# Transposing normalized activations in square blocks on VectorE and through memory instead of on TensorE, in two layers of attention and feed-forward

## The chip, the cores and the metric

The kernel runs on one core of a Trainium2 chip. The engines are TensorE (PE, with its weight loads PEld), VectorE (DVE), ScalarE (ACT), GpSimd (POOL) and SyncE (SP, which issues most transfers here). The metric is the device time of one execution in microseconds, lower is better. All sizes below are in fp32.

## The reference

Two rounds of attention and a SwiGLU feed-forward, each behind a layer normalization and with a residual. There are S = 2048 tokens of D = 448 features; 16 heads of 28 features share one key and one value (multi-query); the feed-forward is 1792 wide.

```
def _A_ref(x, wq, wk, wv, wo):
    q = (x @ wq).reshape(B, S, 16, 28).transpose(0, 2, 1, 3)
    k, v = x @ wk, x @ wv
    scores = einsum("bhqd,bkd->bhqk", q, k) * 28 ** -0.5
    o = einsum("bhqk,bkd->bhqd", softmax(scores), v)
    return o.transpose(0, 2, 1, 3).reshape(B, S, 448) @ wo
def _B_ref(x, w_gate, w_up, w_down):
    return (silu(x @ w_gate) * (x @ w_up)) @ w_down
for _ in range(2):
    x = x + _A_ref(layernorm(x), ...)
    x = x + _B_ref(layernorm(x), ...)
```

## The kernel before

**Layout.** The residual stream `xres` stays on the chip: 128 partitions (tokens) by 16 tiles by 448 features. Four tiles make a chunk `c` of 512 tokens. Normalization gives `xn`, tokens on partitions; the products need features on partitions, so each chunk is transposed ("turned"). A number is held as a high part and a remainder (`xh`, `xl`; so are weights, `wgh` and `wgl`, `wdh` and `wdl`), and most products are three matmuls. The fourth block of features is half empty; its upper 64 partitions hold a remainder, and for the feed-forward a second copy `xd` holds the high part there.

**The turn.** `norm_steps` (L207 to L230) gives nine steps for a chunk: statistics of four tiles, one reciprocal root on GpSimd, and four normalizations on VectorE (L226, 128x448 each). `flip` (L238) then runs, for each of four blocks of features, four transpositions of 128x128 on PE (L243) into one PSUM bank, and `flipped` (L246) copies the bank to `xh` on ScalarE (L249, L256, L257) and subtracts to `xl` on VectorE (L250, L259). With four chunks, two layers and two products that is 16 turns of 16 transpositions, 256 in all.

**The order.** The order in which the program is written is each engine's order. The names of the stages, with the times of layer 0:

- *Projection* (`project` L458, `q` L478): sixteen products (`product_T` L261, eleven matmuls each, L269), four a chunk. Each result goes through ScalarE (`stage`) to memory (`qd`, `kt`); VectorE transposes the piece that holds V (L502); after every fourth, `maxima` (L390) bounds the scores, with its own matmuls (L395) and VectorE steps (L397 to L406).
- *Attention* (`scores` L525): 16 groups of four heads (i = 0 to 15, chunk i // 4), each of 16 steps kt over the key tiles. A step has the score matmuls (L562), two exponentials on ScalarE (L568 for one head, L569 for three) and the products with V (L599). The stacked queries of group i + 2 are brought by `stack` (L372, kt = 4), split by `parts` (kt = 7) and completed by `rows` (kt = 9), into one of three buffers `qstack`. At kt = 10 of groups 4, 8 and 12 `between_steps` (L572) does the output projection (`outproj` L541) of the chunk before: 48 matmuls. In groups 8 and 12, halves of the turn of chunk 0 (for the feed-forward) stand among them.
- *Feed-forward* (`FeedForward`, `unit` L788): the hidden width is seven groups of two blocks (`gi`, `n`), and each block runs over four chunks: 56 units in each layer, 112 in all. A unit has 21 pairs of gate and up matmuls on two halves of the array (L289) in two halves, A and B; the SiLU on ScalarE (L822), the product with `up` on VectorE (L823), the high part on ScalarE (L824), its remainder on VectorE (L827). Between A and B stands the first half of the unit before's `down` (L699, six pairs), and behind B the second. Half B starts when ScalarE has copied one column of A's banks (`between` L293, tile `seen`). `accumulate` (L728) adds the finished sums of a chunk to `xres`: two on VectorE (L736), two by a ScalarE copy to `stage` (L739) and a GpSimd addition (L740).
- *Around the feed-forward's start* (`rest` L853): chunk 1 is turned behind the last output projection, chunks 2 and 3 in halves inside units (`mid`: at gi = 0, (c, n) = (1, 1) and (2, 1)).
- *Around its end* (`hand_over` L754): as soon as a chunk is finished its statistics are taken and, through the list `soon` (each entry counts units), its normalization. Chunks 0 and 1 are turned for the next attention inside the units of chunks 2 and 3, the first three projections run behind units, and the rest behind the last one, with the turns of chunks 2 and 3.

Two tiles with one buffer link these: `xn`, and `sg`, which the SiLU and `maxima` both use.

Of the kernel before, what the change touches and what calls it, by code (L numbers as in the profile page):

```python
# [8 lines left out]
F32 = mybir.dt.float32  # L9
# [6 lines left out]
P = 128  # L16
# [13 lines left out]
LEAD = 4  # L30
# [23 lines left out]
def forward(  # L54
# [28 lines left out]
    xpool = ctx.enter_context(tc.tile_pool(name="xpool", bufs=1))  # L83
# [47 lines left out]

    def split(hi, lo, raw):
        nc.gpsimd.tensor_scalar(hi, raw, 1.0, 0.0, ALU.mult, ALU.add)
        nc.gpsimd.tensor_tensor(lo, raw, hi, ALU.subtract)
# [9 lines left out]
    qts = [pers.tile([P, 2, 512], F32R, name=f"qstack{n}") for n in range(3)]  # L144
# [62 lines left out]
    def norm_steps(c, pool=pers):  # L207
# [14 lines left out]
        def apply(t):  # L222
            if t == 0:
                got["x"] = pool.tile([P, 4, 512], F32, name="xn")
            o, i, r = got["x"][:, t, 0:D], xres[:, 4 * c + t, :], got["r"][:, t : t + 1]
            nc.vector.tensor_scalar(o, i, mv[:, 4 * c + t, 0:1], r, ALU.subtract, ALU.mult)  # L226
# [3 lines left out]
        return fs + [lambda t=t: apply(t) for t in range(4)], got  # L230

    def norm(c, pool=pers):
        fs, got = norm_steps(c, pool)
        for f in fs:
            f()
        return got

    def flip(got, tiles, ks=range(4), place=None):  # L238

        for k in ks:  # L240
            pt = place if place is not None else bank(wide[-1])[1]
            for t in range(4):
                nc.tensor.transpose(pt[:, P * t : P * t + P], got["x"][:, t, P * k : P * k + P], ident)  # L243
            flipped(tiles, k, pt, nc.vector.tensor_copy if place is not None else nc.scalar.copy)
# [55 lines left out]
    class Attention:  # L300


        def __init__(self, layer):
# [12 lines left out]
            for i in range(3):  # L316
                self.at(4 + 3 * i, lambda i=i: self.stack(i))
                self.at(6 + 3 * i, lambda i=i: self.parts(i))
                if not full:
                    self.at((10, 12, 13)[i], lambda i=i: self.rows(i))  # L320
            if not full:
                self.at(2, self.first_keys)
                self.at(3, self.diagonal)
            for i in range(len(GR) if full else 0):
                fs, place = self.max_steps(i)
                if i == 1:
                    fs[KC] = lambda f=fs[KC]: (f(), self.places[0]())
# [51 lines left out]
        def parts(self, i):  # L379
            q = qts[i % 3]  # L380
            split(q[:, 0, :], q[:, 1, :], qraw)

        def rows(self, i):
# [3 lines left out]
            dst = qts[i % 3][28:125:32, :, :].rearrange("j z (b w) -> j (z b) w", w=32)  # L387
# [31 lines left out]
        def max_steps(self, i):  # L419

            got = {}
            q = qts[i % 3]
# [86 lines left out]
        def finish(self):  # L509
# [12 lines left out]
            self.advance(len(self.steps), NM + KC * LEAD)  # L522
            wide.append(LOW)

        def scores(self, ff):  # L525
            next(switch)
            with tc.tile_pool(name=f"at{self.layer}", bufs=1, reuse_waits="tile") as wp:
# [13 lines left out]
                def outproj(c, t, po, gs=range(NG)):  # L541
                    oh, ol = on[c]
                    ts_ = slice(P * t, P * t + P)
                    for g in gs:
                        for z, (a, b) in enumerate(((oh, woh), (oh, wol), (ol, woh))):
                            nc.tensor.matmul(  # L546
                                po[:, 0:D], a[:, g, ts_], b[:, g, :], start=(g + z == 0), stop=(g == NG - 1 and z == 2)
# [6 lines left out]
                def step(n):  # L554
# [3 lines left out]
                    q, k, ks = qts[i % 3], keys[kt // 4], slice(P * (kt % 4), P * (kt % 4) + P)  # L558
# [13 lines left out]
                def between_steps(n):  # L572
# [3 lines left out]
                    if full:  # L576
                        self.lent = free[:, 0, :]
                        self.advance(KC)
                        if kt == 11 and i + 1 < len(GR):
# [4 lines left out]
                    ks = list({8: (0, 1), 12: (2, 3)}.get(i, ()))  # L584
# [54 lines left out]

                X0 = xtile(xpool)  # L640
                fs, got = norm_steps(0)
                fs1, got1 = norm_steps(1)
                ff.norms[1] = got1
                ff.second = norm_steps(2)
# [318 lines left out]
```

## Time and profile before

| | |
|---|---|
| median of 3 runs | 2031.24 us (2031.08 to 2032.20) |
| the profiled execution's own time | 2031.19 us |
| its span in the trace | 2029.5 us |
| start and first projection | 0 to 64 us |
| attention 0 | 64 to 586 |
| feed-forward 0 | 586 to 1043 |
| second projection | up to 1070 |
| attention 1 | 1070 to 1592 |
| feed-forward 1 and the end | 1592 to 2029.5 |

Busy time in the whole span, from the page:

```profile
PE 2011.8 (99%) x18631; PEld 1274.4 (63%) x18631; DVE 460.7 (23%) x892; ACT 1310.3 (65%) x2152; POOL 535.6 (26%) x599
```

A row of the timeline has the start in the span, the duration, the engine, the line, the operation, the tile written and those read, the shape, a count (rows that follow each other are joined), and in brackets the idle time before it with what ended it. A row of one line's view has the count, the least, median and greatest duration in ns, the first and last start, and the shapes. A row of the windows has start and end, the length, then the busy time and count of PE, PEld, DVE, ACT and POOL, the granted clock, the DMA share and GB/s. PE counts as busy whenever a matmul is under way, so its 99% in the attention doesn't say that it sets the pace there.

### The profile page before, as it was taken

Reading aid. Unit: us, or ns where it says so; the run is one execution under the profiler, and the core shown is the slowest. Engines: PE = TensorE matmul, PEld = TensorE weight load, DVE = VectorE, ACT = ScalarE, POOL = GpSimd, SP = SyncE. Lnnn points to the kernel's source line nnn. Section 1 sums busy time; section 2 is a strip of 40 time slices with the busy share of each in tenths; the row PEclk is TensorE's granted clock in tenths of the full one; section 3 lists DMA queues with packets and bytes.
Section 4 is the critical chain, followed back from the end, with each engine's and each line's share of the span. In section 5 each row is a group of like instructions: output and inputs, shape, how many; then the busy total and the mean of one; then the engine's idle time right before and its main releaser. Section 6 shows DMA issues by size and latency. Waiting matters only on the chain.

```text
span 2029.5 us, 43649 instructions
## 1 busy us (share of the span) xinstructions
PE 2011.8 (99%) x18631; PEld 1274.4 (63%) x18631; DVE 460.7 (23%) x892; ACT 1310.3 (65%) x2152; POOL 535.6 (26%) x599
## 2 busy tenths in 40 slices
PE   9999999999999999999999999999999999999998
PEld 7433434334358999999883343343343689988886
DVE  7200101002115232322451001010011232232322
ACT  4899797997964333333349998979979543333332
POOL 4222211032312333333351221211232123233320
PEclk9999999999999999999999999999999999999999
DMA  5111000011100111100031010000110000111101
GB/s 162 51 30 30 12 22 12 20 28 30 28 12 19 31 31 31 31 25 18 22 99 39 20 30 12 22 12 22 31 47 9 28 16 16 31 31 31 31 1 74
DMA packets 76512, 63.44 MB, mean 31 GB/s; under 512 B 22904, under 2 KB 63224, under 8 KB 76312
## 3 DMA queue, kind: packets, MB, share of 16 engines
q1 hardware_dynamic: 75896, 60.33, 10.8%
q8 instruction: 147, 2.41, 0.5%
q14 instruction: 53, 0.43, 0.1%
q10 hardware_dynamic: 416, 0.26, 0.0%
HBM read 47.72 MB, written 12.32 MB: 30 GB/s over the span
## 4 chain that ended last, share of the span: by engine, by line
PE 48%; ACT 47%; DVE 2%; issue 1%; DMA 1%; POOL 0%; SPq 0%; ACTq 0%; DVEq 0%; POOLq 0%
PE bank L289 39%; ACT pt L569 31%; ACT pt L568 15%; PE bank L269 3%; PE three L546 2%; PE bank L546 2%; PE bank L243 1%; PE bank L599 0%; PE three L562 0%; DMA qd<-stage 0%; DVE xl L250 0%; DVE xn L226 0%; DMA wq<-in_A_wq_dram 0%; DMA kt<-stage 0%; DVE vt L502 0%
## 5 line engine op out<-in xcount | busy, mean ns | idle before, releaser
L569 ACT ACTIVATE pt<-three 128x1536 f32<-128x1536 f32 x512 | 741.3, 1448 | 0.0
L599 PE MATMUL bank<-pt,vsb 128*32 128x512 f32 x4096 | 545.1, 604 | 0.5 <-ACT pt L569 0.5
L562 PEld LDWEIGHTS three<-qstack,keys 32*128 32x128 f32 x4608 | 252.2, 183 | 446.6 <-ACT pt L568 394.1
L562 PE MATMUL three<-qstack,keys 32*128 32x512 f32 x4608 | 497.2, 425 | 0.9 <-DVE vt L502 0.9
L562 PE MATMUL bank<-qstack,keys 32*128 32x512 f32 x1536 | 491.5, 425 | 0.4 <-ACT pt L568 0.4
L289 PE MATMUL bank<-xh,wgh 64*128 64x512 f32 x1728 | 445.3, 390 | 0.4
L289 PE MATMUL bank<-xh,wgl 64*128 64x512 f32 x1404 | 366.7, 390 | 0.0
L568 ACT ACTIVATE pt<-bank 128x512 f32<-128x512 f32 x512 | 306.1, 598 | 68.0 <-PE bank L562 66.7
L289 PE MATMUL bank<-xl,wgh 64*128 64x512 f32 x1296 | 333.3, 390 | 0.0
L289 PE MATMUL bank<-wdh,h 64*128 64x448 f32 x1792 | 330.6, 364 | 1.2 <-ACT h L824 0.8
L289 PEld LDWEIGHTS bank<-xh,wgh 64*128 64x128 f32 x1728 | 261.8, 184 | 18.8 <-DVE xl L250 1.5
L740 POOL TENSOR_TENSOR xres<-stage,xres 128x448 f32<-128x448 f32 x108 | 127.6, 1205 | 497.6 <-ACT stage L739 497.6
L633 POOL TENSOR_TENSOR o<-o 128x512 f32<-128x512 f32 x32 | 41.1, 1285 | 816.3 <-DMA o<-rd 710.5
L289 PEld LDWEIGHTS bank<-wdh,h 64*128 64x128 f32 x1792 | 242.1, 184 | 14.6 <-issue 2.7
L562 PEld LDWEIGHTS bank<-qstack,keys 32*128 32x128 f32 x1536 | 243.3, 183 | 1.1 <-ACT pt L568 1.0
L296 ACT COPY seen<-bank 128x1 f32<-128x1 f32 x664 | 81.5, 163 | 247.7 <-PE bank L289 245.3
L289 PEld LDWEIGHTS bank<-xh,wgl 64*128 64x128 f32 x1404 | 215.9, 184 | 13.7
L289 PE MATMUL bank<-wdl,h 64*128 64x448 f32 x896 | 216.5, 366 | 0.0
L822 ACT ACTIVATE sg<-bank 128x512 f32<-128x512 f32 x112 | 67.3, 601 | 219.7 <-PE bank L289 214.5
L289 PEld LDWEIGHTS bank<-xl,wgh 64*128 64x128 f32 x1296 | 195.6, 184 | 9.8
L599 PEld LDWEIGHTS bank<-pt,vsb 128*32 128x32 f32 x4096 | 80.8, 108 | 189.7 <-issue 174.9
L823 DVE TENSOR_TENSOR sg<-bank,sg 128x512 f32<-128x512 f32 x112 | 77.5, 692 | 500.0 <-ACT sg L822 491.0
(115 smaller groups left out, 1731.6 us busy)
## 6 DMA issues: line engine op xcount, KB each, us to landing
o<-rd SPq DMA_DIRECT2D x32, 256.0 KB
qd<-stage SPq DMA_DIRECT2D x32, 224.0 KB
qraw<-qd SPq DMA_DIRECT2D x128, 56.0 KB
wdr<-in_B_w_down_dram SPq DMA_DIRECT2D x28, 224.0 KB
wr<-in_B_w_gate_dram SPq DMA_DIRECT2D x28, 192.0 KB
wr<-in_B_w_up_dram SPq DMA_DIRECT2D x28, 192.0 KB
out_dram<-xres SPq DMA_DIRECT2D x15, 224.0 KB
xres<-in_A_x_dram SPq DMA_DIRECT2D x3, 896.0 KB
```

The costliest lines, as they stand in the source:

```text
L269: nc.tensor.matmul(po, a, b, start=(i == 0), stop=(i == len(seq) - 1))
L289: nc.tensor.matmul(po, a, b, start=start, stop=stop, skip_group_check=True)
L296: nc.scalar.copy(seen[:, i : i + 1], po[:, 0:1])
L546: nc.tensor.matmul(po[:, 0:D], a[:, g, ts_], b[:, g, :], start=(g + z == 0), stop=(g == NG - 1 and z == 2))
L562: nc.tensor.matmul(three[:, j, :] if j < 3 else one, k[js, kp, ks], q[js, part, :], start=(z == 0), stop=(z == 2), tile_position=(32 * j, 0),)
L568: nc.scalar.activation(pt1, one, AF.Exp, scale=SCALE)
L569: nc.scalar.activation(pt, three, AF.Exp, scale=SCALE)
L599: nc.tensor.matmul(accs[i][32 * j : 32 * j + 32, :], vsb[:, kt, :], pts[n][j], start=(kt == 0), stop=(kt == NT - 1), skip_group_check=True,)
L633: nc.gpsimd.tensor_tensor(rb, oraw, rb, ALU.mult)
L740: nc.gpsimd.tensor_tensor(r, s, r, ALU.add)
L822: nc.scalar.activation(sg, pg[0], AF.Silu)
L823: nc.vector.tensor_tensor(sg, pg[1], sg, ALU.mult)
```

## The change

- **The turn through VectorE and memory.** `norm_steps(c, True)` normalizes a tile into `sg`, and VectorE's transpose turns it in square blocks of 32 by 32 into `xn`, writing every fourth element (16 bytes), so that the four tiles interleave. `send` writes `xn` to memory in four pieces, which puts the blocks in their places, and `load` reads it back with features on partitions. `cut` makes `xh` and `xl` from that with the copies and subtractions of `flipped`, from SBUF instead of PSUM. It is used for all feed-forward chunks of both layers and for chunks 0, 1 and 2 of attention 1: 11 of the 16 turns. The four of attention 0 and chunk 3 of attention 1 stay on PE.
- **Where its steps stand.** For the feed-forward, chunks 0, 1 and 2 are normalized and sent in groups 5, 9 and 13 of the attention and loaded in the next group; 0 and 1 are also cut there, all on VectorE. Chunk 2 is cut in `rest`, chunk 3 goes through `soon` (one unit apart: normalize and send, load, cut). At the hand-over, chunks 0 and 1 go through `soon` in the same way, chunk 2 is loaded behind projection 4 and cut behind projection 6. Two projections run one unit later than before, the third behind the last unit. `mid` is gone.
- **Token order.** Inside a chunk, column 4 p + t now is token 128 t + p. The down products and the output projection take their tokens as every fourth column (`tokens`), and the remaining `flip` writes PSUM so.
- **Buffers.** Two `qstack` instead of three: the stack of group i + 1 is read at kt = 2, split at 5, completed at 9. Two buffers in `xpool` (chunks 0 and 1) instead of one, two in `xbp` instead of three.

The branch with `full` is not taken in the runs, and its edits are left out.

```diff
+    def tokens(cols, t):
+        return cols[:, t:512:4]
...
-    qts = [pers.tile([P, 2, 512], F32R, name=f"qstack{n}") for n in range(3)]
+    qts = [pers.tile([P, 2, 512], F32R, name=f"qstack{n}") for n in range(2)]
...
         def apply(t):
+            o = pers.tile([P, 512], F32, name="sg") if away else None
             if t == 0:
-                got["x"] = pool.tile([P, 4, 512], F32, name="xn")
-            o, i, r = got["x"][:, t, 0:D], xres[:, 4 * c + t, :], got["r"][:, t : t + 1]
+                got["x"] = pers.tile([P, 4, 512], F32, name="xn")
+            o = (o if away else got["x"][:, t, :])[:, 0:D]
+            i, r = xres[:, 4 * c + t, :], got["r"][:, t : t + 1]
             nc.vector.tensor_scalar(o, i, mv[:, 4 * c + t, 0:1], r, ALU.subtract, ALU.mult)
-            nc.gpsimd.tensor_copy(got["x"][:, t, D:512], o[:, 384:D])
+            if away:
+                nc.vector.transpose(side()[:, :, :, t], o.rearrange("p (k s) -> p k s", s=32))
+            else:
+                nc.gpsimd.tensor_copy(got["x"][:, t, D:512], o[:, 384:D])
+        def side():
+            return got["x"].rearrange("p t n -> p (t n)")[:, 0 : 4 * D].rearrange("p (k s t) -> p k s t", s=32, t=4)
+        def send():
+            turns.append(dram.tile([D, 512], F32, name=f"xt{len(turns)}"))
+            got["xt"] = turns[-1]
+            for a in range(4):
+                nc.sync.dma_start(
+                    got["xt"].rearrange("(k r) n -> r k n", r=32)[:, :, P * a : P * a + P],
+                    side()[32 * a : 32 * a + 32].rearrange("p k s t -> p k (s t)"),
+                )
+        def load():
+            got["raw"] = pers.tile([P, 4, 512], F32, name="xn")
+            rows3(got["raw"], got["xt"])
...
+    def cut(got, tiles, ks=range(4), copy=nc.scalar.copy):
         for k in ks:
-            pt = place if place is not None else bank(wide[-1])[1]
+            flipped(tiles, k, got["raw"][:, k, :], copy)
+    def flip(got, tiles):
+        for k in range(4):
+            pt = bank(wide[-1])[1]
             for t in range(4):
-                nc.tensor.transpose(pt[:, P * t : P * t + P], got["x"][:, t, P * k : P * k + P], ident)
-            flipped(tiles, k, pt, nc.vector.tensor_copy if place is not None else nc.scalar.copy)
+                nc.tensor.transpose(tokens(pt, t), got["x"][:, t, P * k : P * k + P], ident)
+            flipped(tiles, k, pt, nc.scalar.copy)
...
-                                po[:, 0:D], a[:, g, ts_], b[:, g, :], start=(g + z == 0), stop=(g == NG - 1 and z == 2)
+                                po[:, 0:D], tokens(a[:, g, :], t), b[:, g, :], start=(g + z == 0), stop=(g == NG - 1 and z == 2)
...
-                        if ks:
-                            flip(got, X0, [ks.pop(0)], one)
...
+                for c in range(3):
+                    ff.X[c] = xtile(xpool) if c < 2 else None
+                    fs, got = norm_steps(c, True)
+                    n = NT * (4 * c + 5)
+                    for kt, f in enumerate(fs):
+                        later[n + 6 + kt] = f
+                    later[n + 18] = got["load"]
+                    for k in range(4) if c < 2 else ():
+                        later[n + 22 + k] = lambda c=c, got=got, k=k: cut(got, ff.X[c], [k], nc.vector.tensor_copy)
...
-                    if kt == 4 and 2 < i + 2 < len(GR):
-                        self.stack(i + 2)
+                    if kt == 2 and i + 1 < len(GR):
+                        self.stack(i + 1)
...
-                                (a[rs, P * t : P * t + P], b[rs, :]),
+                                (tokens(a[rs, :], t), b[rs, :]),
...
             self.soon.append([1, ready])
-            if c < 2:
-                self.mid[len(groups) - 1, c + 2, 0] = [lambda ks=ks: flip(got, a.X[c], ks) for ks in ((0, 1), (2, 3))]
-                self.soon.append([2, lambda: [a.project() for _ in range(2 - c)]])
+            if c == 2:
+                a.plan[4, 1] = [got["load"]]
+                a.plan[6, 1] = [lambda: cut(got, a.X[c])]
+                return
+            self.soon.append([2, got["load"]])
+            self.soon.append([3, lambda: cut(got, a.X[c])])
+            if c == 0:
+                self.soon.append([4, lambda: (a.project(), a.project())])
+                self.soon.append([5, a.project])
...
-            self.turned(1)
-            fs2, self.norms[2] = self.second
-            fs3, self.norms[3] = norm_steps(3)
-            for f in fs2[5:] + fs3[:5]:
+            for c in (0, 1):
+                dma(self.xd[c][64:128, :], self.X[c][0][0:64, 3, :])
+                self.X[c] = (*self.X[c][:2], self.xd[c])
+            third, got = norm_steps(3, True)
+            for f in third[:5]:
                 f()
-            self.soon.append([1, lambda: [f() for f in fs3[5:]]])
             for c in (2, 3):
-                self.mid[0, c - 1, 1] = [lambda c=c, ks=ks: self.turned(c, ks) for ks in ((0, 1), (2, 3))]
+                self.X[c] = xtile(self.xbp, self.xd[c])
+            cut(self.norms[2], self.X[2])
+            self.soon.append([0, lambda: [f() for f in third[5:]]])
+            self.soon.append([1, got["load"]])
+            self.soon.append([2, lambda: cut(got, self.X[3])])
```

The order on VectorE at the end of feed-forward 0, from the last unit's remainder (`h`) to the additions of chunk 3's first two sums (`bank_6650` and `bank_6651` before, `bank_6688` and `bank_6689` after: the banks that the fifth and sixth projections then take), before:

```order
L827 TENSOR_TENSOR h_11683<-sg,h_11683 128x512
L226 TENSOR_SCALAR xn<-xres,mv,rstd 128x448 x4
L502 STREAM_TRANSPOSE vt<-bank_6646 32x512
L365 TENSOR_TENSOR kdiag<-few,mask 112x512
L736 TENSOR_TENSOR xres<-bank_6650,xres 128x448
L736 TENSOR_TENSOR xres<-bank_6651,xres 128x448
```

And in the change (the pair of L232 and L234 stands there four times, once a tile, and is shown once):

```order
L849 TENSOR_TENSOR h_11628<-sg,h_11628 128x512
L525 STREAM_TRANSPOSE vt<-bank_6687 32x512
L277 TENSOR_TENSOR xl<-xn,xh 128x512 x3
L286 TENSOR_TENSOR xh<-xn,xh 64x512
L232 TENSOR_SCALAR sg<-xres,mv,rstd 128x448
L234 STREAM_TRANSPOSE xn<-sg 128x448
...
L525 STREAM_TRANSPOSE vt<-bank_6684 32x512
L388 TENSOR_TENSOR kdiag<-few,mask 112x512
L762 TENSOR_TENSOR xres<-bank_6688,xres 128x448
L762 TENSOR_TENSOR xres<-bank_6689,xres 128x448
```

Chunk 1's four subtractions (L277, L286), four transposes (L234) and one more transpose of V have moved ahead of the two additions.

The order on ScalarE at the start of feed-forward 0, around the third chunk's turn; `bank_78` and `bank_79` are the sums of a finished chunk, the other banks those of gate, up and down. Before, the turn's copies stand behind the first `seen` copies inside the next unit, each half behind its transpositions on PE (the first half shown):

```order
L824 CAST h_7122<-sg 128x512
L739 COPY stage<-bank_78 128x448
L739 COPY stage<-bank_79 128x448
L296 COPY seen<-bank_6647 128x1
L296 COPY seen<-bank_6648 128x1
L249 CAST xh<-bank_6649 128x512
L249 CAST xh<-bank_6646 128x512
L296 COPY seen<-bank_6650 128x1
L296 COPY seen<-bank_6651 128x1
```

And in the change, behind the high part of the unit (gi, c, n) = (0, 2, 0), whose staging copies it also has:

```order
L844 ACTIVATE sg<-bank_6685 128x512
L846 CAST h_7123<-sg 128x512
L765 COPY stage<-bank_78 128x448
L765 COPY stage<-bank_79 128x448
L276 CAST xh<-xn 128x512 x3
L283 CAST xh<-xn 64x512
L284 CAST xd_6851<-xn 64x512
L323 COPY seen<-bank_6687 128x1
L323 COPY seen<-bank_6684 128x1
L323 COPY seen<-bank_6688 128x1
```

All five copies (L276, L283, L284) now stand in one place, ahead of the first `seen` copies of the next unit.

More of the change, by code (lines that the diff above doesn't have):

```diff
@@ L315, in __init__ @@
                 self.at(4 * c + 7, lambda c=c: self.key_split(c))
[L316 to L320, printed above, removed]
+            self.at(4, lambda: self.stack(0))
+            self.at(6, lambda: self.parts(0))
             if not full:
+                self.at(10, lambda: self.rows(0))
                 self.at(2, self.first_keys)
@@ L521, in finish @@
                     f()
-            self.advance(len(self.steps), NM + KC * LEAD)
+            self.advance(len(self.steps), NM)
+            if full:
+                self.places[0]()
             wide.append(LOW)
@@ L670, in scores @@
                         due.pop(n)()
-                    if i in (5, 13, 14) and kt > 5:
-                        for f in {5: fs, 13: fs1, 14: ff.second[0][:5]}[i][kt - 6 : kt - 5]:
-                            f()
+                    if n in later:
+                        later.pop(n)()
                 for n in (last - 2, last - 1):
@@ L906, in forward @@
         nc.sync.dma_start(xres[:, 4 * c : 4 * c + 4, :], xs[:, 4 * c : 4 * c + 4, :])
-    at.X = {c: xtile(xpool if c == 0 else xbp) for c in range(NC)}
+    at.X = {c: xtile(xpool if c < 2 else xbp) for c in range(NC)}
     parts[0]()
```

71 lines of the change are left out of this document (24 added, 47 removed).

## The prediction

> **What bounds the kernel now.** I read the page's chain first, then the busy time by stage, then the rows of single units. The page's lines on the chain that ended last:
>
> ```profile
> PE 48%; ACT 47%; DVE 2%; issue 1%; DMA 1%; POOL 0%; SPq 0%; ACTq 0%; DVEq 0%; POOLq 0%
> PE bank L289 39%; ACT pt L569 31%; ACT pt L568 15%; PE bank L269 3%; PE three L546 2%; PE bank L546 2%; PE bank L243 1%; PE bank L599 0%; PE three L562 0%; DMA qd<-stage 0%; DVE xl L250 0%; DVE xn L226 0%; DMA wq<-in_A_wq_dram 0%; DMA kt<-stage 0%; DVE vt L502 0%
> ```
>
> Two engines share the end: TensorE in the feed-forward (L289), ScalarE's exponentials in the attention (L568, L569). The transpositions (L243) are 1% of the chain, some 20 us. By stage (busy time of PE, PEld, DVE, ACT, POOL with counts; then clock, DMA share, GB/s):
>
> ```profile
> 64.00:586.00 522.00, 519.70 (x5286) 197.62 (x5284) 52.65 (x150) 487.65 (x515) 107.72 (x115) 1.00 0.09 23
> 643.00:984.00 341.00, 341.00 (x3083) 337.18 (x3083) 102.53 (x150) 114.00 (x419) 120.60 (x102) 1.00 0.10 27
> 984.00:1043.00 59.00, 58.63 (x410) 46.08 (x407) 32.06 (x66) 23.78 (x66) 19.30 (x34) 1.00 0.17 49
> ```
>
> The first row is attention 0: ScalarE is busy 487.65 of 522 us. The second is the middle of feed-forward 0: PE has no gap, VectorE is busy 102.53 of 341. The third is its end, where it hands over to attention 1. The granted clock is 1.00 in all three, so work taken from PE is worth its own time, but only where PE is what others wait for. VectorE and the DMA queues have room everywhere on average; what counts is whether they have it at the place.
>
> **The change, part by part.** All sums are against the profiled execution, 2031.19 us, which is the median (2031.24) within 0.05.
>
> *The transpositions that leave PE.* 11 of the 16 turns of a chunk leave it, 176 of 256 transposes. What each is worth is read where it stood. In the attention, halves of one turn stood among the output projections of groups 8 and 12, and none in group 4:
>
> ```profile
> 205.92 0.60 ACT L568 ACTIVATE pt<-bank 128x512 f32<-128x512 f32 x1
> 218.02 0.60 ACT L568 ACTIVATE pt<-bank 128x512 f32<-128x512 f32 x1 [10.16 <-PE bank L562]
> 337.81 0.60 ACT L568 ACTIVATE pt<-bank 128x512 f32<-128x512 f32 x1
> 351.33 0.60 ACT L568 ACTIVATE pt<-bank 128x512 f32<-128x512 f32 x1 [11.57 <-PE bank L562]
> ```
>
> ScalarE idles in both (10.16 and 11.57 us, released by PE), and the step takes 12.10 us without, 13.52 us with half a turn. There are two halves in each layer: 4 x 1.42 = **5.7 us go**. What the change puts there instead (VectorE's normalizations, copies, subtractions of two chunks) is some 20 us on an engine that is busy 52.65 of 522.
>
> At the start of the feed-forward, three turns (chunks 1, 2, 3). The rows are the gate activations of the units, one a unit; the next are two steady ones, then what the chain shows of the first turn and half of the second:
>
> ```profile
> 618.54 0.60 ACT L822 ACTIVATE sg<-bank 128x512 f32<-128x512 f32 x1 [1.96 <-PE bank L289]
> 628.28 0.60 ACT L822 ACTIVATE sg<-bank 128x512 f32<-128x512 f32 x1 [1.29 <-PE bank L289]
> 636.02 0.60 ACT L822 ACTIVATE sg<-bank 128x512 f32<-128x512 f32 x1 [1.96 <-PE bank L289]
> 645.76 0.60 ACT L822 ACTIVATE sg<-bank 128x512 f32<-128x512 f32 x1 [1.29 <-PE bank L289]
> 653.52 0.60 ACT L822 ACTIVATE sg<-bank 128x512 f32<-128x512 f32 x1 [1.68 <-PE bank L289]
> ...
> 697.28 0.60 ACT L822 ACTIVATE sg<-bank 128x512 f32<-128x512 f32 x1 [1.96 <-PE bank L289]
> 704.57 0.60 ACT L822 ACTIVATE sg<-bank 128x512 f32<-128x512 f32 x1 [2.14 <-PE bank L289]
> ```
>
> ```profile
> 609.74 0.45 PE bank L243 x4
> ...
> 612.17 10.08 PE bank L289 x83
> ```
>
> A steady unit is 7.29 us. The four gaps are 9.74, 7.74, 9.74 and 7.76, together 5.82 too long; the first turn holds PE from 609.74 to 612.17, another 2.43. So 8.25 us of each layer hang on turns.
>
> Not all of it is gained, since the third chunk now goes through VectorE, memory and ScalarE behind these very units. The prices:
>
> ```profile
> L226 DVE TENSOR_SCALAR xn<-xres,mv,rstd x64: 500/508/568, 8.3 to 1637.7; 128x448 f32<-128x448 f32 x64
> L397 DVE STREAM_TRANSPOSE sg<-bank x8: 716/717/718, 35.5 to 1071.7; 128x512 f32<-128x512 f32 x8
> L406 DVE STREAM_TRANSPOSE flat<-two x8: 311/311/314, 37.5 to 1075.0; 128x128 f32<-128x128 f32 x8
> L403 DVE CAST two<-ng x8: 215/218/842, 36.9 to 1073.2; 128x64 fp32r<-128x64 f32 x8
> 1027.14 0.69 DVE L827 TENSOR_TENSOR h<-sg,h 128x512 fp32r<-128x512 f32 x1 [0.69 <-ACT h L824]
> 1027.75 1.78 DVE L226 TENSOR_SCALAR xn<-xres,mv,rstd 128x448 f32<-128x448 f32 x4
> 1029.75 0.72 DVE L502 STREAM_TRANSPOSE vt<-bank 32x512 f32<-32x512 f32 x1 [0.21 <-ACT stage L495]
> ```
>
> A square-block transpose costs 311 ns for 128 columns and 717 for 512, so 1.06 ns a column, and 650 ns for 448 if its writes at every fourth element (16 bytes) are free. None of before writes so. The nearest row reads so: L403 takes 64 elements 16 bytes apart in 218 ns. I take 650; the other end is a doubled column time, 1125. Four normalizations follow each other in 1.78 us, so a chunk's eight instructions take 1.78 + 4 x 0.65 = 4.4 us. Behind the unit's own work (L827 stands 2.0 us behind its activation and ends at 2.7; one addition, 0.6) they end 7.7 us behind it. The next unit's product waits for VectorE from 7.29 + 0.6 = 7.9: just in time, and I charge 0.3.
>
> The transfers: a chunk is 224 KB, out in four pieces, in as two. The nearest ones:
>
> ```profile
> 149.81 0.39 SPq L537 DMA_DIRECT2D wr<-in_A_wo_dram  x1
> 152.38 0.94 POOL L133 TENSOR_SCALAR woh<-wr 128x896 fp32r<-128x896 f32 x1 [3.84 <-DMA wr<-in_A_wo_dram]
> 596.38 0.58 SPq L626 DMA_DIRECT2D o<-rd  x1
> 601.62 1.29 POOL L633 TENSOR_TENSOR o<-o 128x512 f32<-128x512 f32 x1 [27.19 <-DMA o<-rd]
> ```
>
> A 98-KB piece is there 2.6 us behind its issue, 256 KB 5.2 us. With four issues of 0.39, out and back are 1.6 + 2.6 + 5.2 = 9.4 us (ends: 1.6 + 2 x 2.6 and 1.6 + 2 x 5.2). Started at 7.7 they land at 17.1 behind the activation. ScalarE wants them two units on, behind its high part and two staging copies, at 14.6 + 2.0 + 1.2 = 17.8: 0.7 to spare.
>
> There stands the cost that I am surest of: ScalarE's five copies (five of 0.59, 3.0 us; the row of L249 below) stand ahead of the one-element copies (`seen`) for which PE's second half waits. PE reaches that half 1.2 + 2.5 + 1.2 = 5.0 us behind an activation (two down halves of six pairs at 0.2, eleven gate pairs at 0.23). ScalarE gets there at 2.0 + 1.2 + 3.0 + 0.3 = 6.5: **1.5 us late**, once a layer. So 8.25 - 0.3 - 1.5 = 6.45 a layer, **12.9 us go**.
>
> ```profile
> L249 ACT CAST xh<-bank x42: 586/591/616, 11.0 to 1648.4; 128x512 fp32r<-128x512 f32 x42
> 704.20 0.54 PE L289 MATMUL bank<-wdh,h 64*128 64x448 f32 x2
> 704.40 0.54 PE L289 MATMUL bank<-wdl,h 64*128 64x448 f32 x2
> L289 PEld LDWEIGHTS bank<-wdh,h 64*128 64x128 f32 x1792 | 242.1, 184 | 14.6 <-issue 2.7 <-ACT h L824 1.2 <-ACT seen L296 1.0
> ```
>
> *The hand-over.* Three turns leave PE here, two in the units of chunks 2 and 3, one in the projection (activations of the units, then the chain):
>
> ```profile
> 981.72 0.60 ACT L822 ACTIVATE sg<-bank 128x512 f32<-128x512 f32 x1 [2.15 <-PE bank L289]
> 991.94 0.60 ACT L822 ACTIVATE sg<-bank 128x512 f32<-128x512 f32 x1 [1.87 <-PE bank L289]
> ...
> 1025.14 0.60 ACT L822 ACTIVATE sg<-bank 128x512 f32<-128x512 f32 x1 [1.97 <-PE bank L289]
> ```
>
> ```profile
> 1026.32 2.72 PE bank L269 x11
> ...
> 1032.33 7.76 PE bank L269 x33
> 1040.09 0.93 PE bank L395 x4
> 1041.02 1.75 PE bank L243 x16
> ```
>
> Each turn in a unit costs 10.22 - 7.29 = 2.9, the third 1.75: 7.6 us raw. But VectorE's order gives most of it back. The fifth projection (before: at 1032.33) waits for the addition that frees its bank, and ahead of that now stand chunk 1's subtractions and chunk 2's normalization and transposes. In the new order the last activation is at 1025.14 - 5.85 - 2.95 (a projection that moved behind it) + 0.3 = 1016.6; down half and third projection end at 1020.5; its staging copy at 1021.1, the first high part at 1021.7. Four subtractions at 0.65 end at 1024.4, the eight instructions at 1028.8, the transpose of V, the key diagonal and the addition (0.72 + 0.69 + 0.62) at 1030.8. So that projection starts 1.5 us earlier, not 5.85. With the third turn 3.3 us go, if chunk 2 is back in time: out from 1028.8, landed at 1038.8, cut by 1041.8, and wanted at 1030.8 + 4 x 2.55 + 0.93 = 1041.9, with nothing to spare. I charge 1.3 and take **2.0 us** (ends: 3.5 gone, 2 added).
>
> *Token order.* PE now loads its stationary tokens at every fourth element, in the down products (12 pairs in each of 112 units, 1344) and the output projections (384 loads), and writes the five remaining turns so. Pairs stand 0.20 us apart; 16 transposes in 1.75 us are 0.109 for 128 columns. A load hides beside the pair until it takes 204/109 = 1.87 times as long. Below that it costs nothing, at twice 1344 x 14 ns + 384 x 15 ns = 25 us, and if the whole record of 184 grew by 109, 156 us. I take nothing, by L403, where elements 16 bytes apart came at full speed. The turns' strided writes lie between nothing and 5 x 1.75 = 8.7 us; I take nothing.
>
> [...] No row of before shows a load of stationary data or a write with that stride.
>
> *Two stacks of queries.* In the attention the next stack is now read behind the last use of the old one, at step 2 of a group, split at 5, completed at 9, and used at 16. Seven steps of 1.9 us remain, 13 us, above the 5.2 of the longest transfer shown: nothing.
>
> **Sum:** 5.7 + 12.9 + 2.0 = 20.6; 2031.19 - 20.6 = **2011 us**.
>
> **Rivals.** (a) *Everything hides*: the raw gains, 5.7 + 16.5 + 7.6 = 29.8, so 2001. For it: VectorE's idle share; against: the two orders above. (b) *The transposes' strided writes take double* (1125 ns): 1.9 us more for each chunk that VectorE has no room for, one at each start and one at the hand-over, 5.7, so 2017. (c) *The transfers come late*: 5.2 each way is 2.6 more, 0.7 of it covered at the starts and nothing at the hand-over: 2 x 1.9 + 2.6 = 6.4, so 2017 as well; with (b) 2023. (d) *Other side, strided stationary loads outgrow their pairs*: the point is 1.87 times; at twice 2036, with doubled writes of the five turns 2045. For it: PEld is busy 337 of 341 us, so there is no slack but the overlap of two row groups; against: L403. [...]
>
> **How the numbers follow.** Forecast 0.42, (a) 0.10, (b) 0.13, (c) 0.13, (d) 0.22: of that 0.17 at twice or worse, 0.05 between 1.87 and 2, near no change. A measurement of this kernel can tell 0.2%, some 4 us. So faster 0.78, the same 0.05, slower 0.17. The range runs from (a), 2001, to the near end of (d), 2036.
>
> **What would show it.** Right: steps of output projection all near 12.1 us; no gap of 9.7 at a feed-forward's start, but one of about 8.8 where ScalarE copies chunk 3; the down pairs still 0.20 apart; L234 (the new transpose) near 650 ns; the fifth projection near 1030.8 less what layer 0 gained before it (2.8 and 6.45), so near 1021.5. Wrong: L234 near 1.1 us (b); ScalarE's or VectorE's cut waiting for a transfer (c); a steady unit longer than 7.29 us (d), which alone would decide the sign.

## The result and the profile after

The changed kernel takes 2121.95 us (median of 4 runs, 2118.87 to 2123.16) against 2031.37: **slower, ratio 1.0443 (95% interval 1.0425 to 1.0461)**. Forecast were 2011 us, in a range of 2001 to 2036. The page's chain and two lines of its groups, after:

```profile
PE 21%; ACT 1%; DMA 1%; DVE 1%; issue 1%; POOL 0%; SPq 0%; POOLq 0%; ACTq 0%
PE bank L316 18%; PE bank L621 1%; ACT pt L593 1%; PE three L586 1%; PE bank L570 1%; PE bank L296 0%; DMA wr<-in_B_w_gate_dram 0%; DVE xn L234 0%; ACT pt L592 0%; DMA xt<-xn 0%; DVE sg L232 0%; DMA qstack<-rows 0%; POOL xres L766 0%; SPq L245 0%; DVE sg L845 0%
...
L586 PE MATMUL three<-qstack,keys 32*128 32x512 f32 x4608 | 502.0, 428 | 16.3 <-DMA qstack<-rows 13.7
...
L316 PEld LDWEIGHTS bank<-wdh,h 64*128 64x128 f32 x1792 | 273.2, 321 | 13.9 <-ACT seen L323 2.7 <-issue 1.1 <-ACT h L846 1.0
```

The chain can be followed for only a quarter of the span this time, but new names stand in it: transfers (`xt`, `qstack`) and VectorE's transpose L234. The score matmuls wait for `qstack`, which they didn't before (the row below is that of before), and a load of stationary tokens takes 321 ns instead of 184.

```profile
L562 PE MATMUL three<-qstack,keys 32*128 32x512 f32 x4608 | 497.2, 425 | 0.9 <-DVE vt L502 0.9
```

The stages that answer to those of before, and four stretches of the hand-over:

```profile
64.00:602.00 538.00, 527.86 (x5274) 205.48 (x5271) 70.88 (x174) 488.42 (x515) 108.41 (x111) 0.99 0.12 34
660.00:1014.00 354.00, 353.53 (x3054) 319.54 (x3056) 93.79 (x147) 108.47 (x421) 122.96 (x102) 0.99 0.09 26
1014.00:1074.00 60.00, 49.03 (x348) 41.64 (x344) 39.20 (x64) 17.68 (x55) 9.76 (x13) 0.93 0.28 79
...
1030.00:1035.60 5.60, 5.54 (x50) 4.89 (x46) 1.44 (x3) 1.93 (x4) 1.10 (x2) 1.00 0.48 156
1035.60:1041.00 5.40, 0.05 (x2) 0.05 (x2) 2.03 (x4) 1.79 (x8) 0.00 (x0) 0.72 0.10 37
1041.00:1044.80 3.80, 3.80 (x18) 3.01 (x20) 3.62 (x6) 0.22 (x4) 0.00 (x0) 0.51 0.01 2
1044.80:1051.80 7.00, 7.00 (x40) 5.59 (x38) 5.98 (x11) 2.24 (x5) 1.44 (x2) 1.00 0.36 82
```

The first attention is 16 us longer with the same ScalarE work (488.42 us), so ScalarE idles more. The steady feed-forward is longer although PE hardly stops in it (353.53 of 354 us). At the hand-over PE is empty for 5.4 us in one piece.

**Where the 90 us are.** From the starts of the SiLU and of the exponentials in both traces: a steady unit is 7.587 us instead of 7.293, times 112 is 33; the attentions are 33 longer, of which 22 are late starts of groups 7, 11 and 15; the feed-forwards' starts 8; from the last unit to the next attention 18. Rounded, that is 92. Two steady units, their down pairs and the first late group:

```profile
703.41 0.60 ACT L844 ACTIVATE sg<-bank 128x512 f32<-128x512 f32 x1 [1.97 <-PE bank L316]
711.00 0.60 ACT L844 ACTIVATE sg<-bank 128x512 f32<-128x512 f32 x1 [1.98 <-PE bank L316]
...
707.32 0.40 PE L316 MATMUL bank<-wdl,h 64*128 64x448 f32 x2
707.55 0.64 PE L316 MATMUL bank<-wdh,h 64*128 64x448 f32 x4
708.02 0.40 PE L316 MATMUL bank<-wdl,h 64*128 64x448 f32 x2
```

Pairs stand 0.23 us apart (707.32 to 707.55; 0.47 for the two in the middle row), not 0.20. In the attention, what SP issues between groups 13 and 15, GpSimd's work and PE's first matmul of group 15:

```profile
542.02 1.84 SPq L400 DMA_DIRECT2D qraw<-qd  x4
543.91 0.39 SPq L128 DMA_DIRECT2D xn<-xt  x1
544.34 0.58 SPq L129 DMA_DIRECT2D xn<-xt  x1
545.02 0.39 SPq L647 DMA_DIRECT2D rd<-rs  x1
553.93 0.58 SPq L648 DMA_DIRECT2D o<-rd  x1
564.39 0.53 SPq L411 DMA_DIRECT2D qstack<-rows  x1
...
559.08 1.29 POOL L655 TENSOR_TENSOR o<-o 128x512 f32<-128x512 f32 x1 [30.34 <-issue]
562.40 0.62 POOL L136 TENSOR_SCALAR qstack<-qraw 128x512 fp32r<-128x512 f32 x1
...
566.54 0.53 PE L586 MATMUL three<-qstack,keys 32*128 32x512 f32 x3 [4.90 <-DMA qstack<-rows]
```

The chunk's load is issued at 543.91. The 8 KB behind it (`rd`, 545.02) let `o<-rd` go only at 553.93, 8.9 us later. GpSimd has the finished group's product (L655) ahead of splitting the next stack (L136), so the split waits too, and PE with it. That the chunk's load is what holds up the 8 KB is here only read from the order of the rows; e11 tests it.

### The profile page after: what moved, and what is told of

Its sections match the earlier page's. It is cut to its first block, busy times and chain, and to the rows that moved or that the text cites. A ratio compares the mean times of both kernels' runs of the same rounds, so it can differ in the third digit from the quotient of the medians.

```text
span 2119.4 us, 43308 instructions
## 1 busy us (share of the span) xinstructions
PE 2056.5 (97%) x18455; PEld 1292.8 (61%) x18455; DVE 494.7 (23%) x944; ACT 1300.1 (61%) x2142; POOL 529.4 (25%) x555
## 5 line engine op out<-in xcount | busy, mean ns | idle before, releaser
L316 PE MATMUL bank<-xh,wgh 64*128 64x512 f32 x1728 | 347.7, 395 | 19.2 <-ACT seen L323 19.2
L316 PE MATMUL bank<-wdh,h 64*128 64x448 f32 x1792 | 318.8, 389 | 2.0 <-ACT seen L323 1.2
L316 PE MATMUL bank<-xh,wgl 64*128 64x512 f32 x1404 | 298.7, 389 | 0.0
L316 PEld LDWEIGHTS bank<-wdh,h 64*128 64x128 f32 x1792 | 273.2, 321 | 13.9 <-ACT seen L323 2.7
L316 PE MATMUL bank<-xl,wgh 64*128 64x512 f32 x1296 | 261.1, 396 | 0.0
L655 POOL TENSOR_TENSOR o<-o 128x512 f32<-128x512 f32 x32 | 41.2, 1286 | 849.6 <-DMA o<-rd 483.3
L323 ACT COPY seen<-bank 128x1 f32<-128x1 f32 x664 | 75.5, 164 | 272.9 <-PE bank L316 272.3
L316 PEld LDWEIGHTS bank<-xh,wgh 64*128 64x128 f32 x1728 | 170.9, 190 | 48.4 <-ACT seen L323 20.1
L316 PE MATMUL bank<-wdl,h 64*128 64x448 f32 x896 | 180.6, 393 | 0.0
L316 PEld LDWEIGHTS bank<-xh,wgl 64*128 64x128 f32 x1404 | 145.8, 187 | 30.3
L634 DVE COPY o<-bank 128x512 f32<-128x512 f32 x32 | 22.1, 691 | 576.8 <-PE bank L621 576.8
```

Of the source, the lines that this page charges most:

```text
L316: nc.tensor.matmul(po, a, b, start=start, stop=stop, skip_group_check=True)
L323: nc.scalar.copy(seen[:, i : i + 1], po[:, 0:1])
L634: nc.vector.tensor_copy(oraw, accs.pop(i))
L655: nc.gpsimd.tensor_tensor(rb, oraw, rb, ALU.mult)
```

## The experiments

Each run is compared with runs of the kernel before on the same chip; "us less" are differences of medians. The kernel before took 2031.37 us beside the change, 2032.39 beside e1 to e4, 2033.79 beside e5 to e7, 2032.08 beside e8 to e10 and 2033.20 beside e11, so a difference between runs of different sets is good to some 2 us.

**e1: the token order alone, on the kernel before.**

```diff
-  nc.tensor.transpose(pt[:, P * t : P * t + P], ...)
+  nc.tensor.transpose(pt[:, t:512:4], ...)
-  a[:, g, P * t : P * t + P]      # output projection; down: a[rs, P * t : P * t + P]
+  a[:, g, t:512:4]                # down: a[rs, t:512:4]
```

> The kernel before with the token order alone: the down products, the output projections and all sixteen turns go by every fourth column; nothing else is changed (what a token is called inside a chunk stays consistent, so nothing is left out). Theory S (the strided stationary loads cost it, 0.294 us a unit and 35 ns a matmul of the output projection, as the trace of the change has them): 112 x 0.294 + 384 x 0.035 = 46 us, so 2077 us, units at 7.59 us, loads near 321 ns. Rival T (the loads were slow only beside the new transfers): units stay at 7.29 us, 2031 us. If the turns' strided writes cost, their 16 transpositions take more than 1.75 us; theory S says they don't.

2080.13 us, ratio 1.0234 (1.0217 to 1.0251): 47.7 us more. Units, and the loads:

```profile
708.76 0.60 ACT L825 ACTIVATE sg<-bank 128x512 f32<-128x512 f32 x1 [1.97 <-PE bank L293]
716.35 0.60 ACT L825 ACTIVATE sg<-bank 128x512 f32<-128x512 f32 x1 [2.15 <-PE bank L293]
...
L293 PEld LDWEIGHTS bank<-wdh,h 64*128 64x128 f32 x1792 | 336.8, 321 | 8.8 <-issue 2.5 <-ACT h L827 1.0 <-ACT seen L300 0.9
...
1065.61 1.75 PE bank L247 x16
```

The unit is 7.59 us and the load 321 ns with no chunk going through memory: theory S. The sixteen strided transpositions (the last row is from the chain) still take 1.75 us, so the strided writes to PSUM cost nothing here.

**e2: the change, with the order undone where a chunk is cut.**

```diff
-  flipped(tiles, k, raw[:, k, :], copy)
+  # copies and subtractions read raw as "p (q t) -> p t q", write xh, xl, xd as "p (t q) -> p t q"
-  return cols[:, t:512:4]
+  return cols[:, P * t : P * t + P]
```

> The change with the order undone where the chunk is cut: the copies and subtractions read the loaded chunk at every fourth element and write the tokens in their old order, so that all stationary loads and the remaining turns are contiguous again. Theory S: units back to 7.29 us, 46 us less, 2076 us, if ScalarE and VectorE read at that stride at full speed (copies still 0.62 and subtractions 0.69 us). Rival: strided reads take as long as the strided writes of the transpose (half as long again), then copies near 0.9 us and 1 to 2 us come back per cut that ScalarE has no room for, some 2081 us. The waits for transfers in the attention and at the hand-over stay in both.

2088.05 us, ratio 1.0272 (1.0255 to 1.0289): 33.9 us less than the change, and less gained than either forecast said. Units are back at 7.293 us, but not all of the 47.7 comes back. The copies of this run, by form (least, median, greatest ns), and then those of the change:

```profile
L280 ACT CAST xh<-xn x21: 1087/1102/1132, 622.8 to 1699.9; 128x512 fp32r<-128x512 f32 x21
L280 ACT CAST xh<-bank x15: 577/592/619, 11.9 to 1090.7; 128x512 fp32r<-128x512 f32 x15
L280 DVE CAST xh<-xn x12: 615/644/675, 271.7 to 1455.4; 128x512 fp32r<-128x512 f32 x12
...
L276 ACT CAST xh<-xn x21: 612/617/625, 626.3 to 1716.0; 128x512 fp32r<-128x512 f32 x21
L276 DVE CAST xh<-xn x12: 419/421/429, 272.9 to 1468.6; 128x512 fp32r<-128x512 f32 x12
```

Strided reads are dear too: 1102 ns on ScalarE, where the change's contiguous ones took 617, and 644 ns on VectorE instead of 421.

**e3: the change with three stacks and the timing of before; e4: the kernel before with two stacks and the change's timing.**

```diff
 e3                                           e4
-  qstack for n in range(2)                   -  qstack for n in range(3)
+  qstack for n in range(3)                   +  qstack for n in range(2)
-  stack, parts, rows (i + 1) at 2, 5, 9      -  stack, parts, rows (i + 2) at 4, 7, 9
+  stack, parts, rows (i + 2) at 4, 7, 9      +  stack, parts, rows (i + 1) at 2, 5, 9
```

With the number of buffers goes the number of stacks that are brought ahead of the first group, three in e3 and one in e4.

> The change with three buffers of stacked queries and the timing of before (group i + 2 at steps 4, 7 and 9); everything else as in the change. Theory B (the attention's stalls come of the two buffers: the small transfers of a finished group wait behind a chunk of 896 KB out and 1 MB in, GpSimd waits for them ahead of splitting the next stack, and the group starts late): the 28 us of stalls at the starts of groups 7, 11 and 15 go, 2094 us. Rival D (the transfers themselves delay what the running group needs, whatever the buffers): the stalls stay, 2122 us.

> The kernel before with two buffers of stacked queries and the change's timing (group i + 1 at steps 2, 5 and 9), nothing else. Theory B (two buffers are enough while no chunk is moved through memory; the stalls need both): 2031 us, no group starts late. Rival (two buffers are too few by themselves): up to 28 us more, 2059 us, with late starts at every group rather than at 7, 11 and 15 alone.

e3: 2097.56 us, 1.032 (1.0302 to 1.0337), 24.4 less than the change, and groups 7, 11 and 15 start on time. e4: 2031.15 us, 0.9993 (0.9984 to 1.0003). Neither the two stacks (e4) nor the chunk's way through memory (e3) makes these late starts alone; together they do.

**e11: the change, with the load behind the small transfers.**

```diff
-  later[n + 18] = got["load"]      # cuts at n + 22 + k
+  later[n + 26] = got["load"]      # cuts at n + 38 + k
```

> The change (two stacks, everything else as it is), but in the attention the load of a chunk stands at step 10 of its group, behind the small transfers that bring the finished group's sums and the next stack, instead of at step 2 ahead of them; the cuts follow 16 steps later. Theory Q (the 1 MB load is what the small transfers wait behind): most of the 24 us of late starts goes, 2098 to 2105 us. Rival (the 896 KB on their way out, issued at the group's end, are what delays them): the late starts stay, 2115 to 2122 us.

2097.31 us, 1.0313 (1.0296 to 1.033): 24.6 less, with two stacks still. SP at the same place:

```profile
541.62 0.35 SPq L647 DMA_DIRECT2D rd<-rs  x1
545.22 0.59 SPq L648 DMA_DIRECT2D o<-rd  x1
555.76 0.56 SPq L411 DMA_DIRECT2D qstack<-rows  x1
556.36 0.48 SPq L128 DMA_DIRECT2D xn<-xt  x1
```

`o<-rd` goes 3.6 us behind `rd`, not 8.9. So it is the load of 1 MB ahead of the small transfers, not the 896 KB on their way out: theory Q. In the change the DMA share is 0.90 from 546 to 548 us, and then only 0.13 to 0.18 until 553: for five of its 8.9 us the small transfer waits while little is moved, which comes back below.

**e5: both cures (e2 and e3 together).** The edits are those two.

> The change with both cures, the order undone where a chunk is cut and three stacks of queries. If the two causes are separate, their gains add up: 33.9 and 24.4 off 2121.95, 2064 us. Rival (the stalls hide part of the slow loads, or the reverse): 2070 us or more. What is left against before, some 32 us, is then in the starts of the feed-forwards (10 and 11 us at the unit that waits for chunk 3's transfer) and at the hand-over and projection (some 17 us).

2062.25 us, 1.0139 (1.0122 to 1.0156): 59.7 less than the change, where the sum of the two was 58.3. So the gains add up, the causes are separate, and 28 us against the kernel before are still open.

**e6: as e5, but only chunks 0, 1 and 2 of the feed-forward go through memory** (six turns in all).

```diff
-  fs, got = norm_steps(c, c < NC - 1)        # hand-over
+  fs, got = norm_steps(c)                    # and turns, projections in units as before
-  third, got = norm_steps(3, True)           # send, load, cut through `soon`
+  third, self.norms[3] = norm_steps(3)       # turned in halves in unit (0, 2, 1) as before
```

> As the run with both cures, but only the feed-forward's chunks 0, 1 and 2 go through VectorE and memory, in the attention, where there is time; chunk 3 and the hand-over's chunks are transposed on PE as before (192 transposes stay, 64 less 16 ... that is 6 of 16 turns leave PE). Theory L (what is lost in the tight places is the time of a chunk's way through memory, out 896 KB and back 1 MB, which no two units cover): the 16 us at the feed-forwards' starts and the 17 us at the hand-over are gone, and the gain of the attention's halves (5.7 us) and of chunks 1 and 2 at the two starts (2 x 5.3 us) shows: 2031 - 16 = 2015 us, up to 2020 with the small stalls that three stacks left (2 to 4 us a layer). Rival (the transfers cost the attention as much as the turns did): 2031 us or more.

2022.01 us, **0.9943 (0.9927 to 0.996): faster than before**, 40.2 less than e5 and a little above what was expected. (160 of the 256 transpositions stay on PE; the 192 of the expectation is a miscount.) The output projection of group 8 has lost its halves of a turn:

```profile
338.81 0.60 ACT L598 ACTIVATE pt<-bank 128x512 f32<-128x512 f32 x1
350.85 0.60 ACT L598 ACTIVATE pt<-bank 128x512 f32<-128x512 f32 x1 [10.09 <-PE bank L592]
```

12.04 us, against 12.10 for the step without a half before.

**e8: e6 and chunk 3 through memory; e9: e6 and the hand-over through memory.** Each is one of e6's two edits left out.

> The run with chunks 0, 1 and 2 in the attention (2022 us), and chunk 3 of the feed-forward through memory as well, as in the change; the hand-over stays on PE. From the rows of the two runs that differ in both, the five units behind the feed-forward's start are 60.6 and 61.6 us long with chunk 3 through memory and 51.7 with it on PE: 8.9 and 9.9 more, 2041 us. Rival (the transfer is late only because the hand-over's or the weights' transfers crowd it in that run): under 2030 us.

> The run with chunks 0, 1 and 2 in the attention (2022 us), and the hand-over's chunks 0, 1 and 2 through memory as in the change; chunk 3 of the feed-forward stays on PE. What is left of the 40 us between the two earlier runs: 40.2 - 18.8 = 21 us more, 2043 us. Rival (the two tight places share a cause, so that one alone costs more than its share): 2050 us or more.

2039.27 us (1.0034, 1.0022 to 1.0047) and 2043.47 us (1.0056, 1.0039 to 1.0072): 17.3 and 21.5 more than e6, together 38.8 of the 40.2; each against its own runs of the kernel before, 19.0 and 23.2, together 42.1. Both bring the strided copies of e2 with them (1.09 us each), which the change itself doesn't have.

**e7: as e6, but nothing on the chip goes by every fourth element.**

```diff
-  nc.vector.transpose(side()[:, :, :, t], o.rearrange("p (k s) -> p k s", s=32))
+  nc.vector.transpose(got["x"][:, t, 0:D], o)
-  4 transfers of 224 KB in runs of 512 bytes; cut reads strided
+  16 transfers of 56 KB in runs of 128 bytes, one for each a and t; cut reads contiguous
```

> As the run before it, but VectorE writes its blocks side by side instead of at every fourth element, and the transfer out puts the tokens in order in runs of 128 bytes, in 16 pieces of 56 KB. Theory W (the writes at every fourth element make the transpose 1.01 us instead of 0.65, and the strided reads of the cut make its copies 1.1 us instead of 0.62): the transposes take 0.65 us and the copies 0.62. The time: about the same as the run before it if the shorter runs are hidden in the attention; 5 us more or worse if 16 issues on SP and the slower transfer delay the small transfers of a group. Rival to W (the transpose of 448 columns costs 1.0 us however it writes): it stays at 1.0 us.

2016.38 us, **0.9919 (0.9902 to 0.9935), the fastest here**, 5.6 less than e6, which was not expected. The transpose in the change and here:

```profile
L234 DVE STREAM_TRANSPOSE xn<-sg x44: 965/994/1123, 251.5 to 1701.8; 128x448 f32<-128x448 f32 x44
```

```profile
L234 DVE STREAM_TRANSPOSE xn<-sg x24: 645/645/648, 250.9 to 1523.6; 128x448 f32<-128x448 f32 x24
...
251.57 11.51 SPq L246 DMA_DIRECT2D xt<-xn  x16
```

Theory W: 645 ns, as the prediction priced it. The sixteen issues hold SP for 11.5 us (the change's four took 3.04 in the row shown below), which three stacks cover.

**e10: e7 with two stacks and the change's timing** (the edit of e4).

> The fastest run so far (short runs, 2016 us) with two stacks of queries and the change's timing. Theory B (two stacks and a chunk on its way through memory in the attention together make the late starts): the six chunks in the attention are all here, so most of the 24 us comes back, 2035 to 2040 us, with late starts of groups 7, 11 and 15. Rival (with no strides on VectorE the chunk is sent early enough): 2016 to 2020 us.

2050.7 us, 1.0088 (1.0071 to 1.0105): 34.3 more than e7, with late starts of groups 7, 11 and 15. Theory B again, and more than was expected. SP's longer row of issues stands ahead of the small transfers as well; whether that is the reason was not tested (`o<-rd` follows `rd` by 9.0 us, as in the change).

## Why the prediction was wrong, step by step

- **"A load hides beside the pair until it takes 204/109 = 1.87 times as long ... I take nothing, by L403."** The first step that failed, worth 47.7 us alone (e1). Rival (d) had the mechanism. The record of a load grew by 137 ns, from 184 to 321; if all of that belongs to the 109 ns of its columns, as the prediction's sum has it, the load takes 246 ns, 2.26 times as long, and the point is passed. No run varies the stride, so the point itself is not tested. The price at twice was 14 ns a pair and 15 a matmul of the output projection. Measured are 24.5 (0.294 us over 12 pairs) and 35 (a step of 13.80 us against 12.10, over 48), so 46 us, not 25. The row I leaned on could not carry it: 64 elements in 218 ns are mostly the fixed cost of an instruction. Rows of before show that for instructions of two operands. L404 reads 64 elements 16 bytes apart, L622 reads 16 contiguous ones, L250 512:

```profile
L622 DVE TENSOR_TENSOR fine<-fine,under x64: 174/175/177, 103.3 to 1600.1; 128x16 f32<-128x16 f32 x64
L404 DVE TENSOR_TENSOR two<-ng,two x8: 264/270/1361, 37.2 to 1073.6; 128x64 fp32r<-128x64 f32 x8
L250 DVE TENSOR_TENSOR xl<-bank,xh x48: 678/690/693, 11.9 to 1649.0; 128x512 fp32r<-128x512 f32 x48
```

  A contiguous element costs (690 - 175)/496 = 1.04 ns, so some 158 ns are fixed, and a strided one costs (270 - 158)/64 = 1.7 ns (estimates from these rows). That is 1.7 times as much, for VectorE's reads: a warning against "nothing", though still under the 1.87, and no price for PE's loads, which by the estimate above grew by more. At every fourth element of SBUF the runs show longer records in loads of stationary data (184 to 321 ns, e1), VectorE's writes (645 in e7, 994 in the change) and ScalarE's reads (617 in the change, 1102 in e2). The strided writes to PSUM in the transpositions of e1 show none: 1.75 us for 16 either way.
- **"A chunk is 224 KB, out in four pieces, in as two."** The second: 224 KB is one piece. A chunk is 448 x 512 x 4 bytes, 896 KB, and comes back as 1 MB, in pieces of 768 and 256 KB. The way of 9.4 us is 16.4 at the start of feed-forward 0, and PE waits for it:

```profile
642.47 3.04 SPq L245 DMA_DIRECT2D xt<-xn  x4
648.78 0.39 SPq L128 DMA_DIRECT2D xn<-xt  x1
649.21 0.58 SPq L129 DMA_DIRECT2D xn<-xt  x1
...
653.45 1.66 ACT L276 CAST xh<-xn 128x512 fp32r<-128x512 f32 x3 [1.66 <-DMA xn<-xt]
658.92 0.62 ACT L283 CAST xh<-xn 64x512 fp32r<-64x512 f32 x1 [3.81 <-DMA xn<-xt]
660.47 0.79 PE L316 MATMUL bank<-xh,wgh 64*128 64x512 f32 x2 [6.30 <-ACT seen L323]
```

  From 642.47 to 658.92. The issues take 3.0 us (1.6 forecast), the load follows 3.3 us later, and its last piece is there 10.1 us behind the first issue of the load, where 5.2 were forecast from another transfer of 256 KB. It is the smaller piece that is late: the 768 KB are there 4.7 us behind their issue, the 256 KB 9.7. The weights' transfers, which are issued right behind it here, are not needed for that. At the hand-over SP issues nothing between 1031 and 1045 us, and the same piece takes 9.5 us (1030.70 to 1040.16); from 1036 to 1039 the DMA share is 0.13, as much as two of the sixteen engines, at 49 to 51 GB/s, where 408 were reached from 1033 to 1034. Why this piece runs so was not tested. The margin of 0.7 us had no chance. Rival (c) named this wait, and priced it at 6.4 us in all.

  The charge of 0.3 beside it failed too: **"The next unit's product waits for VectorE from 7.29 + 0.6 = 7.9: just in time, and I charge 0.3."** What waits is the SiLU itself, since it writes `sg`, which the transposes still use, and the unit takes 9.80 us instead of 7.59:

```profile
642.54 0.60 ACT L844 ACTIVATE sg<-bank 128x512 f32<-128x512 f32 x1 [4.19 <-DVE xn L234]
```

  Instead of 12.9 gained at the two starts, chunk 3's way costs 17.3 against its turn on PE (e8).
- **"Two stacks of queries ... Seven steps remain, 13 us, above the 5.2 of the longest transfer shown: nothing."** Worth 24.4. True without a chunk on its way (e4). What I missed is the chain of work between: the 8 KB behind the chunk's load, GpSimd's product behind that, the split behind the product.
- **The hand-over, "2.0 us".** The order was read rightly and the sizes were not: it costs 21.5 instead (e9). The rows of the change point to L234 at 1.0 us and to the late load. ScalarE's copy of the last block waits for the load, and PE's second half for ScalarE; then the SiLU waits for `sg`, which VectorE's transposes still hold (a link by buffers that I had left out); then the fifth projection for the addition behind them:

```profile
1040.16 0.62 ACT L280 CAST xh<-xn 128x512 fp32r<-128x512 f32 x1 [3.61 <-DMA xn<-xt]
1047.87 0.60 ACT L844 ACTIVATE sg<-bank 128x512 f32<-128x512 f32 x1 [6.65 <-DVE xn L234]
...
1040.95 0.79 PE L316 MATMUL bank<-xh,wgh 64*128 64x512 f32 x2 [5.41 <-ACT seen L323]
1075.50 0.79 PE L296 MATMUL bank<-xh,wh 128*128 128x512 f32 x1 [6.66 <-DVE xres L762]
```

  The run e9, with contiguous loads and three stacks, has the same three waits, of 6.02 us (PE for `seen`), 7.04 (the SiLU) and 6.74 (the fifth projection). How the 21.5 us divide between the slow transposes, the late load and the order was not run.
- **"I take 650; the other end is 1125."** 994 where the writes are strided, 645 where not (e7): rival (b) in kind, 344 ns more where it priced 475.
- **What held.** The attention's halves of a turn were worth what they took (12.04 us steps in e6). With the causes removed and the tight places left to PE, moving turns to idle VectorE pays: 17.4 us in e7 (2016.38 against 2033.79), where the same terms of the prediction, the halves and the turns of chunks 1 and 2, came to about 16. By the starts of the SiLU in the traces, each feed-forward's start gained 5.4 us, as forecast, and the first attention 2.9; of the second attention's 2.8 only 0.3 is left with the hand-over counted in. That is 14.0 us between the two traces, whose executions are 13.5 us apart, so the closeness of 17.4 and 16 is in part chance.

What was not run by itself: why e2 gains 33.9 and not 47.7. By the starts of the SiLU and of the exponentials, the two feed-forwards' starts take some 3 us more than the change's without its slow loads, the way from the last unit to the second attention 2, and the late groups of the first attention 3. The strided reads explain the direction; their share is argued from the rows only, and some 6 of the 14 us are not placed at all.

## What to carry to other kernels

Price a stride only after the fixed cost of an instruction is taken out, by rows of different length (here some 158 ns, the estimate above), and price the loads of stationary data against the spacing of matmuls: the pairs stood 0.20 us apart here, and 0.23 with the strided loads. Count a transfer's bytes from its shape, and follow what stands behind it, on its queue and then on the engine that waits for those small transfers: moving one load eight steps later (and its cuts sixteen) was worth 24.6 us. The detour through memory paid here in the attention (17.4 us in e7), where some 20 us lie between its first issue and the first cut (251.57 to 271.31 in e7), and cost more than it saved in the places of two short units (17.3 us in e8, 21.5 in e9).

## What the runs showed of the hardware

PE came back slow from its stalls at the hand-over. In the windows above it is empty from 1035.6 to 1041.0; in the next 3.8 us the granted clock is 0.51, and only then 1.00. So a wait of 5.4 us cost nearly 2 us more (an estimate: 3.8 us at half the clock). Behind the wait of 6.66 us before the fifth projection the clock is 0.58 from 1075.5 to 1079.5, and 1.00 from 1079.5 to 1081.

Runs of 128 bytes in a transfer were no loss where there was time: e7 took 5.6 us less than e6, although it makes twelve more issues on SP for each chunk. Three things differ between the two (the transposes, the copies and the transfers), and their shares were not run; some 1.9 us in each layer are at the unit behind chunk 2's cut, 17.66 us between two activations instead of 19.60.
